# The second product of the second MoE with w2 as the stationary operand

## The chip, the cores and the metric

The kernel runs on one core of one Trainium2 chip. The metric is the device time of one execution in microseconds (us). The core has a matrix engine (PE, with its weight loads shown apart as PEld), a vector engine (DVE), a scalar engine (ACT), GpSimd (POOL) and a sync engine (SP), which here issues all DMAs.

## The reference

Three layers follow one another: a gated linear attention over 4 batches, 8 heads and 768 positions, a first MoE with one expert (d_ff 2048, gelu by a sigmoid), and a second MoE with four experts of width 1024. There are 3072 tokens of width 384. The change is in the second MoE:

```
p = domain_probs / (domain_probs.sum(-1, keepdims=True) + 1e-09)
for e in range(E):
    h = np.maximum(x @ w1[e], 0.0)
    out += p[:, e:e + 1] * (h @ w2[e])
```

The expert weight p is a number per token and expert. It can be multiplied into the result of the second product, as the reference writes it, or into the relu result before it.

## The kernel before

All products are made of a high and a low part of each float32 operand (both of type float32r), so that one product takes three: high by high, high by low, low by high. `split` makes the two parts: ACT copies the source into the high part, another engine subtracts it for the low part.

Three stages follow one another on PE. Stage one is attention in 24 chunks of 128 tokens, interleaved with the first steps of the first MoE and the conversion of its weights by a list written out by hand (`ORDER`); the entry `p` in it calls `pr_load`, which loads the expert weights and normalises them with four small DVE instructions. Stage two is the rest of the first MoE: 64 steps of `L1` (first product, L462) and `L2` (second product, L486), each 9 matmuls of 128 by 128 stationary and 512 tokens moving. Its results go to DRAM (`ydram`) and come back through `y_pieces`.

Stage three is the second MoE, the list `bsteps`: 8 units u (half an expert each, 512 of its 1024 hidden columns), in each 6 blocks j of 512 tokens, in each 4 slices ft of 128 hidden columns, so 192 steps. Step s runs `L3(u, j, ft)` and then `L4` of the step two before it (`lag = 2`; the operands wait in `pend`).

- `L3` (L514): 9 matmuls, w1 stationary, 512 tokens moving, into PSUM bank 3 or 4. Then ACT makes `hi` = relu (L520) and DVE makes `lo` = relu less `hi` (L521), in a ring of four pairs of tiles `G`.
- `L4` (L537): for each of four groups t of 128 tokens, 3 matmuls with `hi` or `lo` of these tokens as the stationary operand and 384 columns of w2 moving: 12 matmuls. The four results of a block have one PSUM bank each, out of a ring of six (`obanks`). With the last slice (ft = 3) DVE multiplies the result by p, a number per partition, and adds it to `acc` (L545 for u = 0, L547 after). In the last unit each group of 128 finished tokens is stored at once (L551).

`acc` holds tokens on the partitions and 384 columns along each. Things that run beside the steps are hung on step numbers by `at(i, fn)`: loads of the unit's weights (`unit_pieces`, L286, through the ring `RAW` of six tiles given out by `raw_tile`) and of `y`. SP issues in the order of its queue; a DMA that must wait for its tile holds up those behind it. The order within each engine's queue is laid down when the program is built, from the program order and the dependencies.

Of the kernel before, what the change touches and what calls it, by code (L numbers as in the profile page):

```python
# [8 lines left out]
F32 = mybir.dt.float32  # L9
F32R = mybir.dt.float32r  # L10
U32 = mybir.dt.uint32
ACTF = mybir.ActivationFunctionType
ALU = mybir.AluOpType
# [4 lines left out]


ORDER = """  # L20
00 10 01 11 20 30 l2 21 31 c0 c1 l3 c2 p c3 c7 c4 02 L c5 12 L L 22 M c6 L c8 03 32 l4 M 04 c9 M
L c10 13 M L 23 c11 M M 33 l5 c12 14 L L L 05 24 c13 34 15 L l6 M 06 L 25 M L M c14 35 M L l7 M
16 c15 L 26 M M 36 07 L L 17 27 M l8 37 M c16 c17 L M L 08 M L L M M L L c18 M L L c20 M M L L
l9 18 c19 M L M L M c23 M L L M M L c21 M L c22 09 M M M 28 38 L L 19 l10 L 010 M 29 39 L M 110
# [174 lines left out]
def attention_moe_moe2_kernel(  # L199
# [11 lines left out]
    nc = tc.nc  # L211
    NCH = qkf.shape[0]
    D = qkf.shape[2]
    NT, DM = out.shape
    NB = NT // 512
    CPB = 6
    NU = w1.shape[0]
    UPE = NU // probs.shape[2]
    KD = DM // 128
# [4 lines left out]
    dram = ctx.enter_context(tc.tile_pool(name="dram", bufs=1, space=bass.MemoryType.DRAM))  # L224
# [3 lines left out]
    arena = const.tile([128, 9224], F32, name="arena")  # L228
    WIDE = [const.tile([128, 1024], U32, name=f"wide{i}") for i in range(3)]
    bank = [psum.tile([128, 512], F32, name=f"bank{i}") for i in range(8)]  # L230
    pend_c = const.tile([128, NCH, 4], F32, name="pend_c")
    worst = const.tile([128, 1], F32, name="worst")
    flag = const.tile([1, 1], mybir.dt.int32, name="flag")
    ydram = dram.tile([NB + 2, KD, 128, 512], F32, name="ydram")
    yrows = [[0, 1], [2, 3]] + [[j + 2] for j in range(2, NB)]

    ident = const.tile([128, 128], F32, name="ident")
# [6 lines left out]
    pr = const.tile([128, NT // 128, 4], F32, name="pr")  # L244
    prs = const.tile([128, NT // 128, 1], F32, name="prs")
# [21 lines left out]
    GF = [carve(512) for _ in range(2)]  # L267
    CV = [[const.tile([128, 512], F32, name=f"cv{i}{j}") for j in range(3)] for i in range(2)]
    RAW = CV[0] + CV[1]
    acc = arena[:, 0:NT // 128 * DM].rearrange("p (a b) -> p a b", b=DM)  # L270

    raw_n = [0]

    def raw_tile():
        raw_n[0] += 1
        return RAW[raw_n[0] % 6]

    def split(hi, lo, src, eng):
        nc.scalar.copy(out=hi, in_=src)  # L279
        eng.tensor_tensor(out=lo, in0=src, in1=hi.bitcast(F32), op=ALU.subtract)  # L280

    def load_split(hi, lo, *srcs):
        def go():
            r = [raw_tile() for _ in srcs]
            for t, src in zip(r, srcs):
                nc.sync.dma_start(out=t, in_=src)  # L286

            def later():
                if len(r) > 1:
                    nc.gpsimd.tensor_tensor(out=r[0], in0=r[0], in1=r[1], op=ALU.add)  # L290
                split(hi, lo, r[0], nc.vector)
            return later
        return go

    def unit_pieces(hi, lo, src):
        return [
            load_split(hi[:, 512 * i:512 * i + 512], lo[:, 512 * i:512 * i + 512],
                       src[:, 512 * i:512 * i + 512])
            for i in range(3)
        ]  # L300
# [200 lines left out]
    onum = [0]  # L501
    obanks = [5, 6, 7, 0, 1, 2]

    def L3(u, j, ft):
        s = step_n[0]
        step_n[0] += 1
        h = bank[3 + s % 2]
        whi, wlo = us[u % 2][0]
        yhi, ylo = ys[j]
        i = 0  # L510
        for w, y in ((whi, yhi), (whi, ylo), (wlo, yhi)):
            for k in range(KD):
                c0 = 512 * k + 128 * ft
                nc.tensor.matmul(  # L514
                    h, w[:, c0:c0 + 128], y[:, 512 * k:512 * k + 512],
                    start=(i == 0), stop=(i == 8),
                )
                i += 1
        hi, lo = G[2 * (s % 4)], G[2 * (s % 4) + 1]
        nc.scalar.activation(out=hi, in_=h, func=ACTF.Relu)  # L520
        nc.vector.scalar_tensor_tensor(  # L521
            out=lo, in0=h, scalar=0.0, in1=hi.bitcast(F32), op0=ALU.max, op1=ALU.subtract
        )
        pend.append((u, j, ft, hi, lo))

    cur = {}

    def L4():
        u, j, ft, hi, lo = pend.pop(0)
        whi, wlo = us[u % 2][1]  # L530
        for t in range(4):
            if ft == 0:
                cur[t] = bank[obanks[onum[0] % 6]][:, 0:DM]
                onum[0] += 1
            o = cur[t]
            for s, (h, w) in enumerate(((hi, whi), (lo, whi), (hi, wlo))):
                nc.tensor.matmul(  # L537
                    o, h[:, 128 * t:128 * t + 128], w[:, DM * ft:DM * ft + DM],
                    start=(ft == 0 and s == 0), stop=(ft == 3 and s == 2),
                )  # L540
            if ft == 3:
                i = 4 * j + t
                p = pr[:, i, u // UPE:u // UPE + 1]
                if u == 0:
                    nc.vector.tensor_scalar_mul(out=acc[:, i], in0=o, scalar1=p)  # L545
                else:
                    nc.vector.scalar_tensor_tensor(  # L547
                        out=acc[:, i], in0=o, scalar=p, in1=acc[:, i], op0=ALU.mult, op1=ALU.add
                    )
                if u == NU - 1:  # L550
                    nc.sync.dma_start(out=out[128 * i:128 * i + 128], in_=acc[:, i])  # L551


    if True:
# [12 lines left out]
        for t in s_bd:  # L567
# [4 lines left out]
            out=mask, in_=mask, pattern=[[1, 128]], compare_op=ALU.is_ge, fill=0.0,  # L572
# [3 lines left out]
        for g in range(4):  # L576
            for (hi, lo), w in ((win[g], w_in[g]), (wout[g], w_out[g])):
                for i in range(3):
                    c0 = slice(512 * i, 512 * i + 512)
# [7 lines left out]
        def weights(n):  # L587
            for _ in range(min(n, len(wq))):
                hi, lo, src = wq.pop(0)
                r = WIDE[wide_n[0] % 3]  # L590
                nc.sync.dma_start(out=r, in_=src.bitcast(U32))
                loaded.append((wide_n[0], hi, lo, r))
                wide_n[0] += 1
# [7 lines left out]
        def convert(n):  # L601
            for _ in range(min(n, len(loaded))):
                convert_a()
                weights(1)
                hi, lo, w = half.pop(0)
                split(hi, lo, w, engine("weight_lo", conv_n[0]))
                conv_n[0] += 1

        def pr_load():
            nc.sync.dma_start(out=pr, in_=probs)  # L610
            nc.vector.reduce_sum(out=prs, in_=pr, axis=mybir.AxisListType.X)
            nc.vector.tensor_scalar_add(out=prs, in0=prs, scalar1=1e-9)
            nc.vector.reciprocal(out=prs, in_=prs)
            nc.vector.tensor_tensor(
                out=pr, in0=pr, in1=prs.to_broadcast([128, NT // 128, 4]), op=ALU.mult
            )

        weights(3)
        for _ in range(12):
            nc.tensor.matmul(bank[4][:, 0:128], ident, ident, start=True, stop=True)  # L620
# [5 lines left out]
        for ev in ORDER:  # L626
            if ev[0] == "c":
                convert(1)
            elif ev == "p":
                pr_load()  # L630
            elif ev == "L":
                L1(*esteps.pop(0))
            elif ev == "M":
                L2()
            else:
                acts[ev[0]](int(ev[1:]))()
# [4 lines left out]
        def at(i, fn):  # L641
            side.setdefault(i, []).append(fn)
# [20 lines left out]
        def piece_at(i, go):  # L663
            cell = []
            at(i, lambda: cell.append(go()))
            at(i + 2, lambda: cell[0]())

        e = len(steps) - 16
        for i, go in enumerate(unit_pieces(*us[0][0], w1[0])):
            piece_at(e + i, go)  # L670
        for i, go in enumerate(unit_pieces(*us[0][1], w2[0])):
# [6 lines left out]
        for i, (j, f, t0, n) in enumerate(steps):  # L678
# [7 lines left out]
            out=worst, in_=pend_c, axis=mybir.AxisListType.XY, op=ALU.min  # L686
# [3 lines left out]
            out=worst[0:1], in_=bank[5][0:1, 0:128], axis=mybir.AxisListType.X, op=ALU.min  # L690
        )
        nc.vector.tensor_scalar(
            out=flag, in0=worst[0:1], scalar1=PMIN, scalar2=None, op0=ALU.is_le
# [7 lines left out]
        for u in range(1, NU):  # L701
            pieces = unit_pieces(*us[u % 2][0], w1[u]) + unit_pieces(*us[u % 2][1], w2[u])
            for i, go in enumerate(pieces):
                piece_at(24 * (u - 1) + 6 + 2 * i + (4 if u == 1 else 0), go)
        lag = 2
        for i, (u, j, ft) in enumerate(bsteps):
            L3(u, j, ft)
            for fn in side.pop(i, []):
                fn()
            if len(pend) > lag:  # L710
                if len(pend[0]) == 6:
                    L2()
                else:
                    L4()
        while pend:
            L4()
# [53 lines left out]
```

## Time and profile before

| | |
|---|---|
| median of 3 runs | 1359.32 us (1358.34 to 1360.66) |
| profiled execution | 1360.01 us |
| its span, first to last instruction | 1358.3 us |
| mean granted TensorE clock | 0.984 of full speed |
| first matmul of L514, last matmul of L537 | 543.43 us, 1351.13 us |

The columns of a timeline are start and duration in us, engine, line, operation, result from operands, count; what stands in brackets is the idle time of that engine before and what ended it. Neighbouring instructions of one group are merged in one line. A matmul's duration is longer than the distance to the next one, since matmuls overlap in the array: what a group of matmuls takes is the distance between the starts of two groups, not its duration.

### The profile page before, as it was taken

The page shows a single profiled execution, that of the slowest core. Times are in us where ns is not written, and L with a number is a line of the kernel's source. Part 1 is how long each engine was busy: PE and PEld are TensorE (multiplying, and loading weights), DVE is VectorE, ACT ScalarE, POOL GpSimd, SP SyncE. Part 2 cuts the span into 40 slices and gives each one's busy share as a digit, 9 for nine tenths or more (in the row PEclk, how much of TensorE's full clock was granted, in tenths as well). Part 3 has the DMA queues.
Part 4 walks back from the last instruction along what each step waited for, and adds up shares of the span by engine and source line. Part 5 has one row for each costly group of instructions (what it writes and reads, how often), then busy time and mean ns, then how long its engine had stood idle before and what let it go on. Part 6 is the DMA issues. An engine that isn't in the chain of part 4 may idle for free.

```text
span 1358.3 us, 19558 instructions
## 1 busy us (share of the span) xinstructions
PE 1319.4 (97%) x8297; PEld 1154.7 (85%) x8297; DVE 611.4 (45%) x971; ACT 375.2 (28%) x674; POOL 133.9 (10%) x153
## 2 busy tenths in 40 slices
PE   5887999999999999999999999999999999999997
PEld 4776787888888888899999999999999999999997
DVE  8998367656656354523323323323323333333222
ACT  4664443334333344312112112112112112111111
POOL 5554233101111020000000000000000000000000
PEclk7788999999999999999999999999999999999999
DMA  7454112212111041400100001001001000000111
GB/s 225 138 154 131 39 49 77 75 35 82 52 45 52 1 147 47 156 0 17 31 0 25 23 0 31 17 0 32 16 0 33 15 1 1 1 0 0 36 52 55
DMA packets 30577, 64.32 MB, mean 47 GB/s; under 512 B 4368, under 2 KB 7440, under 8 KB 30480
## 3 DMA queue, kind: packets, MB, share of 16 engines
q1 hardware_dynamic: 30480, 62.98, 15.5%
q8 instruction: 67, 1.10, 0.3%
q14 instruction: 30, 0.25, 0.1%
HBM read 51.95 MB, written 11.01 MB: 46 GB/s over the span
## 4 chain that ended last, share of the span: by engine, by line
PE 84%; DVE 0%; DVEq 0%; issue 0%
PE bank L537 30%; PE bank L514 29%; PE bank L462 11%; PE bank L486 11%; PE bank L436 2%; PE bank L369 1%; PE bank L365 0%; PE bank L397 0%; DVE arena L547 0%; DVEq L719 0%; PE bank L688 0%
## 5 line engine op out<-in xcount | busy, mean ns | idle before, releaser
L537 PE MATMUL bank<-r,g 128*128 128x384 f32 x2304 | 434.8, 337 | 0.0
L514 PE MATMUL bank<-r,r 128*128 128x512 f32 x1728 | 430.7, 393 | 0.0
L537 PEld LDWEIGHTS bank<-r,g 128*128 128x128 f32 x2304 | 409.6, 188 | 16.8
L514 PEld LDWEIGHTS bank<-r,r 128*128 128x128 f32 x1728 | 321.4, 188 | 58.7
L521 DVE SCALAR_TENSOR_TENSOR g<-bank,g 128x512 fp32r<-128x512 f32 x192 | 132.2, 688 | 364.3 <-ACT g L520 364.3
L520 ACT ACTIVATE g<-bank 128x512 fp32r<-128x512 f32 x192 | 114.6, 597 | 615.5 <-PE bank L514 614.7
L486 PE MATMUL bank<-g,r 128*128 128x512 f32 (+1 forms) x936 | 220.4, 381 | 7.5 <-DVE g L280 2.5
L462 PE MATMUL bank<-r,r 128*128 128x512 f32 (+1 forms) x936 | 222.2, 385 | 2.3 <-ACT r L279 1.3
L486 PEld LDWEIGHTS bank<-g,r 128*128 128x128 f32 x936 | 169.9, 193 | 43.7 <-DVE g L280 3.7
L462 PEld LDWEIGHTS bank<-r,r 128*128 128x128 f32 x936 | 168.6, 195 | 37.1 <-issue 1.6
L547 DVE SCALAR_TENSOR_TENSOR arena<-bank,pr,arena 128x384 f32<-128x384 f32 x168 | 95.5, 610 | 132.6 <-PE bank L537 132.6
L470 DVE SCALAR_TENSOR_TENSOR arena<-arena,bank 128x512 f32<-128x512 f32 (+1 forms) x104 | 66.0, 636 | 87.4 <-ACT arena L469 87.3
L469 ACT ACTIVATE arena<-bank 128x512 f32<-128x512 f32 (+1 forms) x104 | 58.6, 564 | 121.3 <-PE bank L462 120.7
L280 DVE TENSOR_TENSOR g<-arena,g 128x512 fp32r<-128x512 f32 (+1 forms) x96 | 69.4, 724 | 40.1 <-ACT g L279 39.1
L279 ACT CAST g<-arena 128x512 fp32r<-128x512 f32 (+1 forms) x104 | 60.9, 589 | 78.5 <-DVE arena L470 78.5
L280 DVE TENSOR_TENSOR r<-cv,r 128x512 fp32r<-128x512 f32 x84 | 61.4, 747 | 45.4 <-ACT r L279 28.4
L279 ACT CAST r<-cv 128x512 fp32r<-128x512 f32 x90 | 54.4, 619 | 82.7 <-POOL cv L50 26.7
L50 POOL TENSOR_TENSOR cv<-cv,cv 128x512 uint32<-128x512 uint32 x24 | 35.5, 1480 | 42.8 <-DVE cv L47 28.9
L369 PE MATMUL bank<-arena 48*128 48x128 f32 x384 | 34.8, 317 | 0.0
L348 DVE TENSOR_TENSOR_SCAN arena<-arena,ends 128x512 f32<-128x512 f32 x24 | 33.8, 1410 | 0.2
L369 PEld LDWEIGHTS bank<-arena 48*128 48x128 f32 x384 | 28.9, 214 | 5.3 <-issue 4.4
L352 POOL TENSOR_TENSOR arena<-arena 128x512 f32<-128x512 f32 x22 | 29.9, 1361 | 15.1 <-DMA arena<-in_qkf 15.1
(70 smaller groups left out, 494.8 us busy)
## 6 DMA issues: line engine op xcount, KB each, us to landing
cv<-in_w SPq DMA_DIRECT2D x48, 256.0 KB, 2.8
arena<-in_qkf SPq DMA_DIRECT2D x48, 192.0 KB, 3.8
arena<-in_v SPq DMA_DIRECT2D x24, 256.0 KB, 3.8
wide<-in_w_in SPq DMA_DIRECT2D x12, 512.0 KB, 4.7
wide<-in_w_out SPq DMA_DIRECT2D x12, 512.0 KB, 4.3
ydram<-cv SPq DMA_DIRECT2D x24, 256.0 KB, 2.2
cv<-ydram SPq DMA_DIRECT2D x24, 256.0 KB, 3.0
arena<-in_qkf SPq DMA_DIRECT2D x48, 96.0 KB, 3.6
```

Source lines behind the costliest of these rows:

```text
L279: nc.scalar.copy(out=hi, in_=src)
L280: eng.tensor_tensor(out=lo, in0=src, in1=hi.bitcast(F32), op=ALU.subtract)
L369: nc.tensor.matmul(ab(c)[1 + r][:, 128 * p:128 * p + 128], kt[64 * r:64 * r + D, p], qt[64 * r:64 * r + D, p], start=True, stop=True,)
L462: nc.tensor.matmul(h, w[:, c0:c0 + 128], x[:, 512 * k + t0:512 * k + t0 + n], start=(i == 0), stop=(i == 8),)
L469: nc.scalar.activation(out=th, in_=h, func=ACTF.Tanh, scale=0.851)
L470: nc.vector.scalar_tensor_tensor(out=gf, in0=th, scalar=1.0, in1=h, op0=ALU.add, op1=ALU.mult)
L486: nc.tensor.matmul(bank[d][:, t0:t0 + n], w[:, c0:c0 + 128], g, start=(f == f0 and s == 0 and t0 == 0), stop=(f == f1 and s == 2 and t0 + ...
L514: nc.tensor.matmul(h, w[:, c0:c0 + 128], y[:, 512 * k:512 * k + 512], start=(i == 0), stop=(i == 8),)
L520: nc.scalar.activation(out=hi, in_=h, func=ACTF.Relu)
L521: nc.vector.scalar_tensor_tensor(out=lo, in0=h, scalar=0.0, in1=hi.bitcast(F32), op0=ALU.max, op1=ALU.subtract)
L537: nc.tensor.matmul(o, h[:, 128 * t:128 * t + 128], w[:, DM * ft:DM * ft + DM], start=(ft == 0 and s == 0), stop=(ft == 3 and s == 2),)
L547: nc.vector.scalar_tensor_tensor(out=acc[:, i], in0=o, scalar=p, in1=acc[:, i], op0=ALU.mult, op1=ALU.add)
```

## The change

In all steps of stage three but the last four (the last block of the last unit), `L4` takes w2 as the stationary operand (128 hidden by 128 output columns) and the 512 tokens of `hi` or `lo` as the moving one: 9 matmuls into 3 banks. The result stands transposed, output columns on the partitions and tokens along them, so p can no longer be a number per partition. It is multiplied into the relu result instead: DVE makes `gf` = relu times p (p spread over all partitions in `wide(.., 0)`), then `split` makes `hi` on ACT and `lo` on DVE. `acc` is kept transposed, with a plain copy or add of 128 by 512.

`pr_make` takes the place of `pr_load`: the same four steps, a transpose on PE and a store to DRAM (`ptd`), at step 48 of 64 of stage two. `pb_load` fetches for each unit and block the 512 weights, repeated on 128 partitions, six steps before the block (48 DMAs).

In the last unit each finished block is turned back: per 128 output columns one DVE transpose of 32 by 32 blocks into a `RAW` tile and four DMAs of 32 partitions, whose runs in DRAM are 32 numbers (128 bytes) long. That is 12 DMAs for each of five blocks. The last block keeps the old form of `L4` (`L4_last`), for which its partial sum of seven units is turned the same way through DRAM (`last_turn` at step 176, 12 DMAs to `otd`; `last_load` at step 182).

```
-    nc.scalar.activation(out=hi, in_=h, func=ACTF.Relu)
+    gf = wide(s, 1)
     nc.vector.scalar_tensor_tensor(
-        out=lo, in0=h, scalar=0.0, in1=hi.bitcast(F32), op0=ALU.max, op1=ALU.subtract
+        out=gf, in0=h, scalar=0.0, in1=wide(NB * u + j, 0), op0=ALU.max, op1=ALU.mult
     )
+    split(hi, lo, gf, nc.vector)
...
+def turned(src, dst, k):
+    r = raw_tile()
+    nc.vector.transpose(r, src)
+    for a in range(4):
+        c0 = 128 * k + 32 * a
+        nc.sync.dma_start(
+            out=dst[:, c0:c0 + 32].rearrange("(b i) c -> i b c", i=32),
+            in_=r[32 * a:32 * a + 32].rearrange("i (b c) -> i b c", c=32),
+        )
...
 def L4():
     u, j, ft, hi, lo = pend.pop(0)
     whi, wlo = us[u % 2][1]
+    if u == NU - 1 and j == NB - 1:
+        L4_last(ft, hi, lo, whi, wlo)
+        return
+    for d in range(KD):
+        if ft == 0:
+            cur[d] = bank[obanks[onum[0] % 6]]
+            onum[0] += 1
+    for s, (w, h) in enumerate(((whi, hi), (whi, lo), (wlo, hi))):
+        for d in range(KD):
+            c0 = DM * ft + 128 * d
+            nc.tensor.matmul(
+                cur[d], w[:, c0:c0 + 128], h,
+                start=(ft == 0 and s == 0), stop=(ft == 3 and s == 2),
+            )
+    if ft < 3:
+        return
+    for d in range(KD):
+        a = acc[:, j, d]
+        if u == 0:
+            nc.vector.tensor_copy(out=a, in_=cur[d])
+        else:
+            nc.vector.tensor_tensor(out=a, in0=a, in1=cur[d], op=ALU.add)
+        if u == NU - 1:
+            turned(a, out[512 * j:512 * j + 512], d)
...
+def pr_make():
+    nc.sync.dma_start(out=pr, in_=probs)
+    nc.vector.reduce_sum(out=prs, in_=pr, axis=mybir.AxisListType.X)
+    nc.vector.tensor_scalar_add(out=prs, in0=prs, scalar1=1e-9)
+    nc.vector.reciprocal(out=prs, in_=prs)
...
+    nc.tensor.transpose(bank[6][0:4 * NT // 128, 0:128], pn, ident)
+    nc.scalar.copy(out=pt, in_=bank[6][0:4 * NT // 128, 0:128])
+    nc.sync.dma_start(out=ptd.rearrange("e (i t) -> (e i) t", t=128), in_=pt)
...
+def pb_load(u, j):
+    def go():
+        nc.sync.dma_start(
+            out=wide(NB * u + j, 0),
+            in_=ptd[u // UPE:u // UPE + 1, 512 * j:512 * j + 512].to_broadcast([128, 512]),
+        )
+    return go
...
+e = len(steps) - 16
+at(e, pr_make)
+for n in range(2):
+    at(e + 12 + n, pb_load(0, n))
...
+for n in range(2, NU * NB):
+    at(4 * n - 6, pb_load(n // NB, n % NB))
+at(4 * NU * NB - 16, last_turn)
+at(4 * NU * NB - 10, last_load)
```

## Rows read from the trace of the kernel before

**Rows 1.** Page, part 1: busy time of each engine.
```profile
PE 1319.4 (97%) x8297; PEld 1154.7 (85%) x8297; DVE 611.4 (45%) x971; ACT 375.2 (28%) x674; POOL 133.9 (10%) x153
```
**Rows 2.** Page, part 4: the chain that ended last, by engine and line.
```profile
PE bank L537 30%; PE bank L514 29%; PE bank L462 11%; PE bank L486 11%; PE bank L436 2%; PE bank L369 1%; PE bank L365 0%; PE bank L397 0%; DVE arena L547 0%; DVEq L719 0%; PE bank L688 0%
```
**Rows 3.** That chain in order of time: start us, us, engine, tile, line.
```profile
821.87 2.10 PE bank L537 x12
...
1181.92 2.10 PE bank L537 x12
```
**Rows 4.** Timeline of PE, 1001.0 to 1006.1: late in stage three.
```profile
1001.73 2.27 PE L537 MATMUL bank<-r,g 128*128 128x384 f32 x12
1003.84 2.24 PE L514 MATMUL bank<-r,r 128*128 128x512 f32 x9
1005.92 0.51 PE L537 MATMUL bank<-r,g 128*128 128x384 f32 x2
```
**Rows 5.** Timeline of PE, 547.6 to 556.0: stage two passes into stage three.
```profile
547.64 2.20 PE L514 MATMUL bank<-r,r 128*128 128x512 f32 x9
549.68 2.20 PE L486 MATMUL bank<-g,r 128*128 128x512 f32 x9
551.72 2.20 PE L514 MATMUL bank<-r,r 128*128 128x512 f32 x9
553.76 2.27 PE L537 MATMUL bank<-r,g 128*128 128x384 f32 x12
555.86 0.39 PE L514 MATMUL bank<-r,r 128*128 128x512 f32 x1
```
**Rows 6.** Windows: stretch, length; busy PE, PEld, DVE, ACT, POOL; clock, DMA share, GB/s.
```profile
0.00:34.00 34.00, 19.60 (x237) 17.02 (x238) 27.68 (x43) 15.81 (x30) 19.56 (x30) 0.80 0.75 225
1001.89:1006.07 4.18, 4.18 (x23) 3.79 (x22) 2.79 (x5) 0.60 (x1) 0.00 (x0) 1.00 0.00 0
1351.50:1355.00 3.50, 0.00 (x0) 0.00 (x0) 0.63 (x2) 0.00 (x0) 0.00 (x0) 1.00 0.66 226
```
**Rows 7.** Groups by line and shape: busy us, mean ns; idle before, releaser.
```profile
L521 DVE SCALAR_TENSOR_TENSOR g<-bank,g 128x512 fp32r<-128x512 f32 x192 | 132.2, 688 | 364.3 <-ACT g L520 364.3
L520 ACT ACTIVATE g<-bank 128x512 fp32r<-128x512 f32 x192 | 114.6, 597 | 615.5 <-PE bank L514 614.7 <-DVE r L280 0.7
L547 DVE SCALAR_TENSOR_TENSOR arena<-bank,pr,arena 128x384 f32<-128x384 f32 x168 | 95.5, 610 | 132.6 <-PE bank L537 132.6
...
L348 DVE TENSOR_TENSOR_SCAN arena<-arena,ends 128x512 f32<-128x512 f32 x24 | 33.8, 1410 | 0.2
```
**Rows 8.** Timeline of all engines, 524.0 to 528.3: after an L1 of stage two.
```profile
525.04 2.20 PE L486 MATMUL bank<-g,r 128*128 128x512 f32 x9
525.30 0.60 ACT L469 ACTIVATE arena<-bank 128x512 f32<-128x512 f32 x1 [2.10 <-PE bank L462]
...
527.50 0.68 DVE L280 TENSOR_TENSOR g<-arena,g 128x512 fp32r<-128x512 f32 x1
```
**Rows 9.** Groups by line and shape: the instructions of pr_load.
```profile
L613 DVE RECIPROCAL prs<-prs 128x24 f32<-128x24 f32 x1 | 0.3, 289 | 0.0
...
L614 DVE TENSOR_TENSOR pr<-pr,prs 128x96 f32<-128x96 f32 x1 | 0.2, 236 | 0.0
L611 DVE TENSOR_REDUCE prs<-pr 128x24 f32<-128x96 f32 x1 | 0.2, 221 | 0.0
...
L612 DVE TENSOR_SCALAR prs<-prs 128x24 f32<-128x24 f32 x1 | 0.2, 164 | 0.0
```
**Rows 10.** DMA issues: what, queue, count, KB each, median us to landing.
```profile
cv<-in_w SPq DMA_DIRECT2D x48, 256.0 KB, 2.8
...
out<-arena SPq DMA_DIRECT2D x24, 192.0 KB, 1.9
```
**Rows 11.** Line 551 by itself: min, median, max ns on SP's queue.
```profile
L551 SPq DMA_DIRECT2D out<-arena x24: 332/332/382, 1271.0 to 1352.4; - x24
```
**Rows 12.** Timeline, 1349.5 to 1358.3: the last results and stores.
```profile
1349.94 2.19 DVE L547 SCALAR_TENSOR_TENSOR arena<-bank,pr,arena 128x384 f32<-128x384 f32 x4 [3.38 <-PE bank L537]
1350.59 2.14 SPq L551 DMA_DIRECT2D out<-arena  x4
```

More of the change, by code (lines that the diff above doesn't have):

```diff
@@ L20 @@
 ORDER = """
-00 10 01 11 20 30 l2 21 31 c0 c1 l3 c2 p c3 c7 c4 02 L c5 12 L L 22 M c6 L c8 03 32 l4 M 04 c9 M
+00 10 01 11 20 30 l2 21 31 c0 c1 l3 c2 c3 c7 c4 02 L c5 12 L L 22 M c6 L c8 03 32 l4 M 04 c9 M
 L c10 13 M L 23 c11 M M 33 l5 c12 14 L L L 05 24 c13 34 15 L l6 M 06 L 25 M L M c14 35 M L l7 M
@@ L234, in attention_moe_moe2_kernel @@
     ydram = dram.tile([NB + 2, KD, 128, 512], F32, name="ydram")
+    ptd = dram.tile([4, NT], F32, name="ptd")
+    otd = dram.tile([512, DM], F32, name="otd")
     yrows = [[0, 1], [2, 3]] + [[j + 2] for j in range(2, NB)]
@@ L269, in attention_moe_moe2_kernel @@
     RAW = CV[0] + CV[1]
-    acc = arena[:, 0:NT // 128 * DM].rearrange("p (a b) -> p a b", b=DM)
+    acc = arena[:, 0:NB * KD * 512].rearrange("p (a b c) -> p a b c", b=KD, c=512)
     raw_n = [0]
@@ L502, in attention_moe_moe2_kernel, with wide @@
     obanks = [5, 6, 7, 0, 1, 2]
+    def wide(i, n):
+        return WIDE[i % 3].bitcast(F32)[:, 512 * n:512 * n + 512]
+    def pr_make():
[3 more added lines that the diff above has]
+        nc.vector.reciprocal(out=prs, in_=prs)
+        pn, pt = wide(2, 0)[:, 0:4 * NT // 128], wide(2, 1)[0:4 * NT // 128, 0:128]
+        nc.vector.tensor_tensor(
+            out=pn.rearrange("p (e i) -> p i e", e=4), in0=pr, in1=prs.to_broadcast([128, NT // 128, 4]),
+            op=ALU.mult,
+        )
[9 more added lines that the diff above has]
+        return go
     def L3(u, j, ft):
@@ L530, in L4, with last_turn, last_load, L4_last @@
         whi, wlo = us[u % 2][1]
+        if u == NU - 1 and j == NB - 1:
[11 more added lines that the diff above has]
+                    start=(ft == 0 and s == 0), stop=(ft == 3 and s == 2),
+                )
+        if ft < 3:
[8 more added lines that the diff above has]
+                turned(a, out[512 * j:512 * j + 512], d)
+    at_last = []
+    def last_turn():
+        for d in range(KD):
+            turned(acc[:, NB - 1, d], otd, d)
+    def last_load():
+        at_last.extend(arena[:, DM * t:DM * t + DM] for t in range(4))
+        for t in range(4):
+            nc.sync.dma_start(out=at_last[t], in_=otd[128 * t:128 * t + 128])
+    def L4_last(ft, hi, lo, whi, wlo):
         for t in range(4):
@@ L541, in L4 @@
             if ft == 3:
[L542 to L551, printed above, removed]
+                r = at_last[t]
+                i = 4 * (NB - 1) + t
+                nc.vector.tensor_tensor(out=r, in0=o, in1=r, op=ALU.add)
+                nc.sync.dma_start(out=out[128 * i:128 * i + 128], in_=r)
     if True:
@@ L607, in convert @@
                 conv_n[0] += 1
[L609 to L616, printed above, removed]
         weights(3)
@@ L628, in attention_moe_moe2_kernel @@
                 convert(1)
-            elif ev == "p":
-                pr_load()
             elif ev == "L":
```

## The prediction

> **What bounds the kernel now.** I read the page's busy times first. PE is busy 97% of the span and no other engine half of it [rows 1], but a busy PE is only a PE with something in its array, so the next view is the chain of work that ended last. There L537 and L514, the two products of the second MoE, hold 59% of the span, and vector work holds next to nothing [rows 2]. In order of time the chain repeats one step without a change: 86 steps lie between 821.87 and 1181.92, so one takes 360.05 / 86 = 4.187 us [rows 3]. PE's timeline splits it by the starts of its groups: 2.11 us for the 12 matmuls of L537 with 384 columns, 2.08 us for the 9 of L514 with 512 [rows 4]. In such a step PE is busy all 4.18 us at a granted clock of 1.00 (2.4 GHz), DVE 2.79 and ACT 0.60 us [rows 6]. So stage three is bound by the rate at which PE takes matmuls. Nothing else in it is worth time unless it stops PE.
>
> The two groups have the same columns: 9 x 512 = 12 x 384 = 4608. A change that keeps columns can only gain what each matmul costs beyond its columns. The passage from stage two to stage three shows this: for two steps L514 still stands beside L486, which already has the form that the change gives to the second product (weights stationary, 512 of the relu or gelu result moving, 9 matmuls into 3 banks). There both groups take 2.04 us (547.64, 549.68, 551.72), 227 ns a matmul; from the first L537 on it is 2.10 us [rows 5]. So L514 is 0.04 us dearer beside the 384-column form than beside the 512-column form, and L537 itself 0.07 us.
>
> A page of the Trainium skill, TensorE: Matmul & The Clock Gate, section "Wait — 56ns, not 53.3ns?", gives a warm matmul its columns at 2.4 GHz and about 2.5 ns. Three matmuls fewer a step would by that be 7.5 ns, an estimate of 1.4 us over 188 steps. The trace does not agree: 227 ns for 512 columns is 13 ns over the 213 ns of the columns.
>
> **The change part by part.**
>
> The product. 192 steps less the last four have the new form: 188. Each falls from 4.187 us to 2 x 2.04 = 4.08 us. That is 0.107 us, times 188 is 20.1 us, all on the path. I take the 4.08 since the same code of L3 ran at it beside the same shape of product. Bounds: if only L4 falls to 2.04 and L3 stays at 2.08, 0.07 x 188 = 13 us; more than 20 is excluded as both groups run at the best pitch seen.
>
> The operands. Now ACT 0.60 and DVE 0.69 us follow a finished L3; after the change DVE 0.69 (relu times p, costed as L521, which also reads the bank and one tile), ACT 0.60, DVE 0.69 [rows 7]. This chain of 2.0 us and hand-offs has four PE groups, 8.2 us, before L4 needs it, and the bank of L3 is free after its first link, earlier than now. Stage two carries a longer chain with the same lag: tanh, product, copy, difference, from 525.30 to 528.18, and its PE goes on without a gap [rows 8]. Cost nothing, covered by those groups. Without that cover it would be 0.7 us a step.
>
> DVE's load. Per block (4 steps) now 4 x 0.69 + 4 x 0.61 = 5.2 us; after it 8 x 0.69 and three adds of 512 columns at 0.69, 7.6 us of 16.3. Copies of unit weights come on top, as now. Nothing on the path.
>
> The spread weights. 48 loads of 256 KB; a load of that size lands in 2.8 us [rows 10], and the step number leaves six steps, 24 us. The tile that each one takes was last read three blocks before, by a step already past when the load comes up, so it does not hold SP's queue for the weight loads behind it. Nothing.
>
> The start. Four DVE instructions, 0.29 + 0.24 + 0.22 + 0.16 = 0.9 us [rows 9], leave a stretch where DVE is busy 27.7 of 34 us and PE 19.6 [rows 6]. DVE is the nearer bound there: between 0 and 0.9 us gained, I take 0.5. Their new place, step 48 of stage two, puts a PE transpose behind them. If PE stands right behind L2 of that step, it waits for the chain of the L1 before it (2.9 us [rows 8]) and these 0.9 us, with 2.0 us of L2 beside it: 1.8 us lost at most, none if the transpose is queued later. I take 0.9. ACT's copy and SP's store of it hold the weight loads behind them by about the same, which step 50 first needs: nothing.
>
> The turning back. DVE transposes of 128 x 512 are not in the trace. The nearest rows are 0.69 us for a pass over two operands and 1.41 us for a scan [rows 7]; I take 0.69, since it is a pass without a running value, and keep 1.41. A block of the last unit then has a burst of 3 x (0.69 + 0.69) = 4.1 us on DVE, with the next step's first link behind it 4.8 us, against the 6.1 us that PE runs before it needs that bank again: nothing. At 1.41 it is 7.0 us, 0.9 us late, six times with the partial sums: 5.4 us. I take 0.5.
>
> The stores. 72 DMAs, each of 512 runs of 128 bytes, 32 per DMA engine if spread over all 16: 2304 runs an engine. They have from the end of the last unit's first block to the last matmul, 18 steps and two products, 78 us. On SP a store takes 0.33 us whatever the size in the trace [rows 11]: 24 us of 78, and the last 12 have 12 us. On the engines the four last stores move 512 packets of 1536 bytes at a share of 0.66 of 3.5 us: 0.66 x 3.5 x 16 / 512 = 72 ns a packet [rows 6]. A run of 128 bytes then costs between 6 ns (by bytes) and 72 ns (by packets). I take 20: 46 us of 78, hidden. Unhidden, it would be added to the end.
>
> The end. L4_last makes the same matmuls, DVE passes and stores as now [rows 12]. Nothing.
>
> Sum: -20.1 - 0.5 + 0.9 + 0.5 = -19.2 us. The profiled execution took 1360.0 us, 1.7 around its span of 1358.3; so 1340.8. The median of the runs shown is 0.7 lower, 1359.3, and gives **1340.1**.
>
> **The rivals.**
>
> *Short runs fill the DMA engines (slower).* At 72 ns a run the 72 stores take 2304 x 0.072 = 166 us, 88 more than they have, and the end waits for the last of them: -19 + 88 = +69, **1428**. It decides from (78 + 19) / 2304 = 42 ns. For it: no run so short is in the trace. Against it: packets of one size cost about their bytes, and a price by packets needs a large fixed part. The Trainium skill speaks for it: DMA: Bandwidth & Descriptors, Specifications, says that below 512 bytes the engine reads, modifies and writes. Doubling my 20 ns for that, an estimate, gives 40, just under that point. No run here shows it.
>
> *SP becomes the bound at the end.* If issuing goes with the number of runs, 512 against 128 is 4 x 0.33 = 1.3 us, 72 of them 96 us, 18 more than 78. The gain is given back: **1359**. At 1.1 us still hidden.
>
> *L3 keeps its 2.08 us.* Gain 13 instead of 20: **1347**. Rows 5 speak against it.
>
> *Only columns count.* Both groups of a step keep their 9216 columns, so w2 as weights could bring the irregular pitch along and both groups still take 4.18 us together; less the 0.9 us at the start and a few tenths the gain is about 1, **1358**. Against it: L486 has the same form and runs at 2.04 us [rows 5]. It is what the rule of the page on TensorE quoted above comes to here.
>
> **How the numbers follow.** Forecast 0.74, L3 keeps its pitch 0.08, SP 0.06, columns 0.04, short runs 0.08. Under 0.2% (2.7 us) is about what a measurement of this kernel cannot tell from none. Faster is the first two and 0.02 of the SP case, where issuing is a little cheaper: 0.84. Same is the rest of SP less 0.01 and the columns: 0.07. Slower is the short runs and that 0.01: 0.09. The range starts at 1336.5: no wait at the new transpose, no late bursts, the full 0.9 at the start, and 2 us for the queues of stage one, which are laid down anew without their entry `p`. It reaches to 1350, which takes in the late DVE bursts (1345) and the L3 rival; 0.18 lies above.
>
> **What would show it.** Right: starts of L3 and L4 groups 2.04 us apart all through stage three, the step 4.08 us, no idle PE in the last unit, the last transposed store landed before the last matmul. Wrong: groups still at 2.08 to 2.11; idle PE released by DVE's `gf` or by a spread-weight load; SP's stores of `turned` at over 1 us each, or a DMA share near 1 from the last unit's first block on with a tail behind the last matmul longer than now.

## The result and the profile after

The changed kernel takes 1340.57 us (median of 4 runs, 1340.32 to 1342.46) where the kernel before takes 1358.93 (median of 4, the three of the table ahead and one more): a ratio of 0.9865, with a 95% interval of 0.9853 to 0.9876. Measured once more in a later set it was 0.9862 [0.9847, 0.9877]. The profiled execution took 1340.8 us and has a span of 1339.1, 19.2 less than before.

The page of the changed kernel, parts 1 and 4, against [rows 1, 2]:

```profile
PE 1298.7 (97%) x7734; PEld 1075.7 (80%) x7734; DVE 737.9 (55%) x1134; ACT 378.8 (28%) x675; POOL 136.1 (10%) x153
...
PE bank L541 29%; PE bank L579 29%; PE bank L464 11%; PE bank L488 11%; PE bank L438 2%; PE bank L371 1%; PE bank L612 1%; PE bank L367 0%; PE bank L399 0%; DVE cv L558 0%; DVE wide L548 0%; DVE arena L619 0%; DVE arena L590 0%; PE bank L749 0%; PE bank L519 0%
```

PE is as busy as before and has 563 matmuls fewer: three in each of 188 steps, less the one transpose that is new. DVE has 126.5 us more to do and is still not in the chain, but for traces: its L548 and L590 now appear, which the rest of this section comes to. L541 is the first product (L514 before), L579 the new second product (L537 before), L612 the old form in the last block.

The timeline of PE in the middle of stage three, against [rows 4]:

```profile
800.57 2.20 PE L579 MATMUL bank<-g,r 128*128 128x512 f32 x9
802.61 2.20 PE L541 MATMUL bank<-r,r 128*128 128x512 f32 x9
804.65 2.20 PE L579 MATMUL bank<-g,r 128*128 128x512 f32 x9
806.69 2.20 PE L541 MATMUL bank<-r,r 128*128 128x512 f32 x9
```

Read the starts: 2.04 us from each group to the next. The step is 4.08 us, and of the 191 distances from one L541 to the next all but the first and the last two have it. From the start of the first matmul of L541 (541.37) to that of the last of L612 (1332.03) there are 790.7 us, where the kernel before had 807.7 (543.43 to 1351.13): 17.0 us less. Another 2.1 us were gained before stage three began, and 0.1 behind the last matmul. These three make the 19.2.

The 17.0 are 188 steps x 0.107 = 20.1 less a loss of 3.0. The loss stands in one place, the timeline of DVE and PE just before the end (what stands in brackets is idle time and what ended it):

```profile
1308.53 2.20 PE L541 MATMUL bank<-r,r 128*128 128x512 f32 x9
...
1312.61 2.20 PE L541 MATMUL bank<-r,r 128*128 128x512 f32 x9
...
1314.65 2.20 PE L579 MATMUL bank<-g,r 128*128 128x512 f32 x9
1316.44 1.28 DVE L590 TENSOR_TENSOR arena<-arena,bank 128x512 f32<-128x512 f32 x2 [7.62 <-PE bank L579]
1317.64 1.30 DVE L558 STREAM_TRANSPOSE cv<-arena 128x512 f32<-128x512 f32 x2
1318.86 1.25 DVE L548 SCALAR_TENSOR_TENSOR wide<-bank,wide 128x512 f32<-128x512 f32 x2
...
1319.57 2.34 PE L541 MATMUL bank<-r,r 128*128 128x512 f32 x9 [2.72 <-DVE wide L548]
```

The first L541 of the last block ends near 1310.6, and its relu pass (L548) could start at once: the spread weights of this block were issued at 1292.55 and had landed at 1297.24. DVE stands idle for 7.62 us instead, since the next instruction in its queue is the add of block 4 (L590), which waits for the L579 that runs from 1314.65. The two relu passes come after two adds and two transposes, at 1318.86, and PE's next L541 needs the bank that the first of them frees. PE starts 2.9 us late. The relu passes were not slow; they were behind.

The new DVE and DMA groups of the changed kernel (groups by line and shape; DMA issues with KB each and median us to landing; line 561 on SP's queue, min, median, max ns):

```profile
L282 DVE TENSOR_TENSOR g<-wide,g 128x512 fp32r<-128x512 f32 x192 | 132.7, 691 | 130.6 <-ACT g L281 130.2
L548 DVE SCALAR_TENSOR_TENSOR wide<-bank,wide 128x512 f32<-128x512 f32 x192 | 132.4, 690 | 247.3 <-PE bank L541 241.4 <-DMA otd<-cv 3.9 <-DMA wide<-ptd 2.0
...
L558 DVE STREAM_TRANSPOSE cv<-arena 128x512 f32<-128x512 f32 x18 | 12.0, 690 | 0.0
```
```profile
wide<-ptd SPq DMA_DIRECT2D x48, 256.0 KB, 3.2
...
out<-cv SPq DMA_DIRECT2D x60, 64.0 KB, 2.0
```
```profile
L561 SPq DMA_DIRECT2D out<-cv x60: 315/502/1430, 1253.5 to 1324.5; - x60
```

And a window over the 12 stores of block 3, issued from 1302.06 to 1309.29 (length; busy PE, PEld, DVE, ACT, POOL; clock, DMA share, GB/s):

```profile
1301.00:1312.00 11.00, 11.00 (x50) 9.09 (x50) 6.07 (x10) 1.25 (x2) 0.00 (x0) 1.00 0.48 73
```

The 12 stores are 6144 runs of 128 bytes. With all other traffic of the window put down to them, 0.48 x 11 us x 16 engines / 6144 is 13.8 ns a run, so a block keeps the engines busy for 5.3 of its 16.3 us.

### The profile page after: what moved, and what is told of

Same layout as the page of the kernel before. It is cut to its first block, busy times and chain, and to the rows that moved or that the text cites. A ratio compares the mean times of both kernels' runs of the same rounds, so it can differ in the third digit from the quotient of the medians.

```text
span 1339.1 us, 18792 instructions
## 1 busy us (share of the span) xinstructions
PE 1298.7 (97%) x7734; PEld 1075.7 (80%) x7734; DVE 737.9 (55%) x1134; ACT 378.8 (28%) x675; POOL 136.1 (10%) x153
## 4 chain that ended last, share of the span: by engine, by line
PE 84%; DVE 0%; issue 0%; DVEq 0%
PE bank L541 29%; PE bank L579 29%; PE bank L464 11%; PE bank L488 11%; PE bank L438 2%; PE bank L371 1%; PE bank L612 1%; PE bank L367 0%; PE bank L399 0%; DVE cv L558 0%; DVE wide L548 0%; DVE arena L619 0%; DVE arena L590 0%; PE bank L749 0%; PE bank L519 0%
## 5 line engine op out<-in xcount | busy, mean ns | idle before, releaser
L541 PE MATMUL bank<-r,r 128*128 128x512 f32 x1728 | 423.2, 389 | 2.7 <-DVE wide L548 2.7
L579 PE MATMUL bank<-g,r 128*128 128x512 f32 x1692 | 414.0, 389 | 0.0
L541 PEld LDWEIGHTS bank<-r,r 128*128 128x128 f32 x1728 | 324.2, 188 | 70.5 <-DVE wide L548 3.1
L579 PEld LDWEIGHTS bank<-g,r 128*128 128x128 f32 x1692 | 317.6, 188 | 65.9
L281 ACT CAST g<-wide 128x512 fp32r<-128x512 f32 x192 | 119.4, 622 | 620.9 <-DVE wide L548 620.9
L548 DVE SCALAR_TENSOR_TENSOR wide<-bank,wide 128x512 f32<-128x512 f32 x192 | 132.4, 690 | 247.3 <-PE bank L541 241.4
L282 DVE TENSOR_TENSOR g<-wide,g 128x512 fp32r<-128x512 f32 x192 | 132.7, 691 | 130.6 <-ACT g L281 130.2
L488 PEld LDWEIGHTS bank<-g,r 128*128 128x128 f32 x936 | 170.2, 193 | 40.1 <-ACT r L281 2.5
L590 DVE TENSOR_TENSOR arena<-arena,bank 128x512 f32<-128x512 f32 x123 | 77.2, 680 | 7.9 <-PE bank L579 7.9
```

The source lines that it names most:

```text
L488: nc.tensor.matmul(bank[d][:, t0:t0 + n], w[:, c0:c0 + 128], g, start=(f == f0 and s == 0 and t0 == 0), stop=(f == f1 and s == 2 and t0 + ...
L541: nc.tensor.matmul(h, w[:, c0:c0 + 128], y[:, 512 * k:512 * k + 512], start=(i == 0), stop=(i == 8),)
L548: nc.vector.scalar_tensor_tensor(out=gf, in0=h, scalar=0.0, in1=wide(NB * u + j, 0), op0=ALU.max, op1=ALU.mult)
L579: nc.tensor.matmul(cur[d], w[:, c0:c0 + 128], h, start=(ft == 0 and s == 0), stop=(ft == 3 and s == 2),)
L590: nc.vector.tensor_tensor(out=a, in0=a, in1=cur[d], op=ALU.add)
```

## The experiments

### Why the old step was dearer than its columns

Of the 0.107 us a step, part must be three matmuls fewer. But 231 ns for each L514 beside 384-column matmuls, against 227 beside 512-column ones [rows 4, 5], is no cost of the second product itself. Three things distinguish the old L4: the width that it moves, the role of its operands (weights that ACT and DVE have just written), and the count of its matmuls. Three kernels set them one by one. The first, from the kernel before:

```diff
-        for t in range(4):
+        for t in range(3):
```

> The kernel before with one of the four token groups of L4 left out (a quarter of the output is not formed): 9 matmuls of 384 columns, with the relu parts as weights. What makes the uneven distances of the old step (L3 at 231 instead of 227 ns a matmul, the first of L4 at 175 to 185 instead of 173)? Theory width (384 moving between 512 moving) and theory role (weights that were just written by ACT and DVE): still uneven, L3 2.08 us, L4 9 x 173 = 1.56 to 1.59. Theory count (12 and 9 matmuls in a step): even, L3 2.04, L4 1.56.

The second, from that one (each of the 9 matmuls moves 512 columns of w2, from a start that stays inside the tile):

```diff
...
-                    o, h[:, 128 * t:128 * t + 128], w[:, DM * ft:DM * ft + DM],
+                    o, h[:, 128 * t:128 * t + 128], w[:, min(DM * ft, 1024):min(DM * ft, 1024) + 512],
...
```

> As g_384, but each matmul of L4 moves 512 columns of w2 (128 of them meaningless): 9 matmuls of 512 with the relu parts as weights. Theory width and theory count: even, L3 and L4 both 2.04 us. Theory role: uneven, L3 2.08 and L4 2.06 to 2.08.

The third, from the changed kernel:

```diff
-                    cur[d], w[:, c0:c0 + 128], h,
+                    cur[d][:, 0:DM], w[:, c0:c0 + 128], h[:, 0:DM],
...
```

> The changed kernel, whose L4 moves only 384 of the 512 tokens (128 tokens of each block are left out): 9 matmuls of 384 with w2 as weights. Theory width: uneven, L3 2.08 us, L4 1.56 to 1.59. Theory role and theory count: even, L3 2.04, L4 1.56.

Measured: 1259.8, 1337.6 and 1270.3 us, a single execution each. The times are those of shorter or longer work; the timelines of PE decide. g_384, g_512 and w_384 in this order:

```profile
801.01 2.24 PE L514 MATMUL bank<-r,r 128*128 128x512 f32 x9
803.09 1.75 PE L537 MATMUL bank<-r,g 128*128 128x384 f32 x9
804.68 0.63 PE L514 MATMUL bank<-r,r 128*128 128x512 f32 x2
```
```profile
800.13 1.07 PE L514 MATMUL bank<-r,r 128*128 128x512 f32 x4
801.04 2.20 PE L537 MATMUL bank<-r,g 128*128 128x512 f32 x9
803.08 2.20 PE L514 MATMUL bank<-r,r 128*128 128x512 f32 x9
```
```profile
800.45 1.75 PE L579 MATMUL bank<-g,r 128*128 128x384 f32 x9
802.04 2.24 PE L541 MATMUL bank<-r,r 128*128 128x512 f32 x9
804.12 1.05 PE L579 MATMUL bank<-g,r 128*128 128x384 f32 x5
```

In g_384 L3 takes 2.08 us and L4 1.59. g_512, with the old roles, 2.04 for L4 and, over the whole stage, steps of 4.08 us: as fast as the change. w_384, with the new roles, has L3 at 2.08 and L4 at 1.59 again. Count falls with g_384 (18 matmuls, uneven), role falls with both others. It is the width. The granted clock is 1.00 from 800 to 808 us in all three.

Whether 384 is dear by itself or only beside 512 took two more kernels, both from w_384. One moves 384 columns in L3 as well:

```diff
...
-                    h, w[:, c0:c0 + 128], y[:, 512 * k:512 * k + 512],
+                    h, w[:, c0:c0 + 128], y[:, 512 * k:512 * k + DM],
...
```

> As w_384, and L3 moves 384 columns too (128 tokens of each block are left out throughout). Theory mix (the uneven distances come from a short product between long ones): even, both groups 9 x 173 = 1.56 us. Rival (384 columns are uneven by themselves): both groups 1.58 us or more.

The other moves 256 in L4 (`h[:, 0:256]` for `h[:, 0:DM]`, and the bank and the add cut likewise):

> As w_384 with 256 columns moving in L4 (half of the tokens are left out). If a matmul costs its columns at 2.4 GHz and 13.3 ns (227 for 512, 173 for 384), L4 takes 9 x 120 = 1.08 us. Theory mix: L3 is uneven again, at 2.08 us or above, since the widths differ more. Rival (something about 384 alone): L3 2.04 us.

Measured: 1167.2 and 1171.6 us, again one execution each, at a granted clock of 1.00 from 800 to 808 us. all_384, then w_256, on PE:

```profile
800.20 1.72 PE L579 MATMUL bank<-g,r 128*128 128x384 f32 x9
801.75 1.72 PE L541 MATMUL bank<-r,r 128*128 128x384 f32 x9
803.32 1.72 PE L579 MATMUL bank<-g,r 128*128 128x384 f32 x9
804.88 0.33 PE L541 MATMUL bank<-r,r 128*128 128x384 f32 x1
```
```profile
800.19 2.00 PE L541 MATMUL bank<-r,r 128*128 128x512 f32 x8
802.02 1.24 PE L579 MATMUL bank<-g,r 128*128 128x256 f32 x9
803.10 2.23 PE L541 MATMUL bank<-r,r 128*128 128x512 f32 x9
```

With one width throughout, 384 is even: 1.56 us for 9, 173 ns each. With 256 in L4 it takes 1.07 us (median), 120 ns each but for the first at 113, and L3 is uneven again at 2.07 (median). So theory mix holds, and each even matmul here costs its columns at 2.4 GHz and 13.3 ns: 213.3 + 13.3 at 512, 160 + 13.3 at 384, 106.7 + 13.3 at 256. The expectation for w_256 had L3 at 2.08 or above; it is 2.07, so a greater difference of widths does not cost more; it costs less.

This divides the gain of a step. The old L4 takes 2.106 us for 12 matmuls and that of g_384 1.586 for 9 (medians): three more cost 0.520, which is 173 ns each, so what unevenness costs does not grow with their count. Three matmuls fewer at 13.3 ns are 0.040 us, 7.5 us over 188 steps; the other 0.067 us, 12.5 us, are the evenness of one width.

### The gap before the last block

> The changed kernel, with the spread weights of the very last block in a tile of their own (floor, unused by then), loaded from step 100. Theory: the 2.9 us that PE stands idle before the last L3 come from DVE's queue, in which the adds of block 4 stand ahead of the first two relu passes of block 5, because the planner expected the load of these weights late; with the load early the relu passes stand first, the gap is gone and the step before last takes 4.08 us: 1337.6. Rival: PE would wait there anyway, for a bank or for the RAW tiles that the stores hold: 1340.6 as now.

```diff
     def wide(i, n):
+        if n == 0 and i == NU * NB - 1:
+            return floor
         return WIDE[i % 3].bitcast(F32)[:, 512 * n:512 * n + 512]
...
-            at(4 * n - 6, pb_load(n // NB, n % NB))
+            at(4 * n - 6 if n < NU * NB - 1 else 100, pb_load(n // NB, n % NB))
```

Measured: 1337.28 us, ratio to before 0.9834 [0.982, 0.9847]. DVE and PE of own_last in the same place:

```profile
1309.59 0.69 DVE L550 SCALAR_TENSOR_TENSOR wide<-bank,floor 128x512 f32<-128x512 f32 x1 [1.96 <-PE bank L543]
...
1313.67 0.69 DVE L550 SCALAR_TENSOR_TENSOR wide<-bank,floor 128x512 f32<-128x512 f32 x1 [1.96 <-PE bank L543]
...
1315.71 1.28 DVE L592 TENSOR_TENSOR arena<-arena,bank 128x512 f32<-128x512 f32 x2
```
```profile
1311.43 2.20 PE L543 MATMUL bank<-r,r 128*128 128x512 f32 x9
1313.47 2.20 PE L581 MATMUL bank<-g,r 128*128 128x512 f32 x9
1315.51 2.20 PE L543 MATMUL bank<-r,r 128*128 128x512 f32 x9
```

Both relu passes now start as soon as their L3 ends, ahead of the adds, and PE runs through. From the start of the first matmul of the stage to that of the last there are 787.6 us instead of 790.7. As the difference is near what runs scatter by, it was measured again beside the changed kernel:

> own_last once more, in one call with the changed kernel itself (the next run), so that both are compared with the same runs of the kernel before. Theory (the gap in DVE's queue is worth 2.9 us): about 3 us under the changed kernel. Rival (the 3.3 us between the first two calls were mostly chance): under 1.5 us.

> The changed kernel without an edit, beside own_last: 1340.6 as before by either theory; the difference to own_last tells.

Measured: 0.9842 [0.9829, 0.9856] against 0.9862 [0.9847, 0.9877]; by the medians 1337.70 against 1339.72. The ratios differ by 0.0020, 2.7 us; their intervals overlap, and it is the traces that show it: 787.6 against 790.7 us in both profiled executions of each. The first theory holds as to the gap: with the relu passes first, PE has nothing else to wait for there. That DVE's queue had its order because the load was expected late is inferred from what the edit does. It is shown that the order changes with the load, whose time and tile the edit changes together; which of the two did it was not separated.

### The stores of short runs

> As own_last, but the 60 stores of the turned blocks are left out (the DVE transposes stay; the first 2560 tokens of the output are not written). Theory: the stores of 128-byte runs are hidden, 13 ns a run on the DMA engines and 0.55 us each on SP: same time as own_last within 0.5 us. Rival: they cost something at the end, through SP's queue or the DMA engines: 1 to 5 us faster than own_last.

From own_last:

```diff
-                turned(a, out[512 * j:512 * j + 512], d)
+                nc.vector.transpose(raw_tile(), a)
```

Measured: 1338.67 us, 0.9845 [0.9832, 0.9859]. It is no faster than own_last; from the first to the last matmul both take 787.6 us. In stage three the stores cost PE nothing. By the medians it is 1.4 us slower. The two profiled executions are 2.2 us apart, and that lies outside stage three: it began 1.0 us later, which is within what it differs by from one execution to another, and the end behind the last matmul was 1.3 us longer, 7.8 us where the executions without doubled stores otherwise have 6.2 to 6.8. What made this end longer was not followed up.

> As own_last, with each of the 60 stores issued twice (the second into a scratch tensor). Theory: the limit is SP's issue, 0.55 us each: 24 a block are 13.2 us of 16.3, and only the last block's group, which has some 12 us to the last result, holds up the final stores: 0 to 4 us slower than own_last. Rival (short runs fill the DMA engines, as in the prediction): 132 stores of 32 runs an engine at 42 ns or more would be 177 us of 78: over 50 us slower. By the 13 ns of the trace they are 55 us and hidden.

Also from own_last:

```diff
...
-            nc.sync.dma_start(
-                out=dst[:, c0:c0 + 32].rearrange("(b i) c -> i b c", i=32),
-                in_=r[32 * a:32 * a + 32].rearrange("i (b c) -> i b c", c=32),
-            )
+            for o in (dst, *more):
+                nc.sync.dma_start(
+                    out=o[:, c0:c0 + 32].rearrange("(b i) c -> i b c", i=32),
+                    in_=r[32 * a:32 * a + 32].rearrange("i (b c) -> i b c", c=32),
+                )
...
```

Measured: 1354.89 us, 0.996 [0.9944, 0.9975]: 17.6 us over own_last, between what theory and rival had. SP, PE and DVE of own_twice, a window, and what SP waited for from 1250 to 1336 us (us in all, times, longest):

```profile
1298.55 0.50 SPq L528 DMA_DIRECT2D wide<-ptd  x1
...
1345.43 1.91 SPq L624 DMA_DIRECT2D out<-arena  x4
```
```profile
1299.55 2.20 PE L583 MATMUL bank<-g,r 128*128 128x512 f32 x9
1305.66 3.91 PE L544 MATMUL bank<-r,r 128*128 128x512 f32 x9 [3.91 <-DVE wide L551]
```
```profile
1301.33 1.88 DVE L594 TENSOR_TENSOR arena<-arena,bank 128x512 f32<-128x512 f32 x3 [6.41 <-PE bank L583]
1303.13 1.89 DVE L561 STREAM_TRANSPOSE cv<-arena 128x512 f32<-128x512 f32 x3
1304.95 1.25 DVE L551 SCALAR_TENSOR_TENSOR wide<-bank,wide 128x512 f32<-128x512 f32 x2
```
```profile
1298.00:1347.00 49.00, 34.44 (x155) 29.13 (x153) 20.21 (x32) 4.95 (x8) 0.00 (x0) 0.89 0.76 128
```
```profile
SPq L565 <- DVE cv L561: 21.8, 4, 8.0
```

SP is occupied almost without a break from 1298 to 1347 and the DMA engines are not (share 0.76). The last matmul starts at 1336.0, the last results leave SP at 1345.4: the end behind the last matmul is 17.4 us instead of 6.6. And at steps 185 and 186 PE loses 5.8 us, in part in the way seen before: the spread weights of block 4 are issued only at 1298.55, behind stores, and land at 1302.26, which is late this time, and DVE has the adds of the block before ahead of the relu passes, which come at 1304.95. So at the end the limit is SP's issue, as the theory had it, but the theory counted the issue alone and left out the waits in its queue: SP stood waiting for DVE's transposes (L561), once for 8.0 us, and the late groups piled up. The rival's price, 42 ns a run or more, is not the one measured (13.8 ns above), and its 50 us or more did not come.

### The start

> The kernel before, with the loading and normalising of the expert weights (four DVE instructions, one DMA) moved from the start to step 48 of stage two; nothing else. Theory: these instructions stand in the way of the DVE-bound start, and their removal is the 2.2 us that the changed kernel is ahead at the end of stage one: first matmul of the second MoE near 541.3 instead of 543.4 us, time near 1356.8. Rival: my step of the prediction, at most 0.9 us of DVE work can be gained: 1358.0 to 1358.9, and the rest of the 2.2 us came in another way.

```diff
-00 10 01 11 20 30 l2 21 31 c0 c1 l3 c2 p c3 c7 c4 02 L c5 12 L L 22 M c6 L c8 03 32 l4 M 04 c9 M
+00 10 01 11 20 30 l2 21 31 c0 c1 l3 c2 c3 c7 c4 02 L c5 12 L L 22 M c6 L c8 03 32 l4 M 04 c9 M
...
         e = len(steps) - 16
+        at(e, pr_load)
```

Measured: 1356.22 us, 0.9975 [0.9964, 0.9986]. PE of p_late where stage three begins:

```profile
540.12 0.27 PE L689 MATMUL bank<-ident,worst 128*1 128x128 f32 x1
540.14 2.33 PE L514 MATMUL bank<-r,r 128*128 128x512 f32 x9
```

Stage three begins at 540.1, where the kernel before had 543.4: the theory's 541.3, and a little more. A single execution says less here than it seems, though. In the profiles of this study stage three begins between 541.8 and 543.4 in the three executions with the early `p`, and between 540.1 and 542.6 in the ten without it. The means, 542.9 and 541.1, are 1.8 apart. The ratio of the runs, 0.9975, is 3.4 us (1.9 to 4.9). Removing 0.9 us of DVE work gains more than 0.9 us. The edit also takes a DMA out of the start and has all queues laid down anew; by which of these, and by which waits, was not followed up.

## Why the prediction was right

The forecast was 1340.1; 1340.57 was measured. Point by point, with the profiled execution's 19.2 us:

- *The product*, -20.1: exact, 188 steps at 4.08 us. The reason was right so far as it went: L514 beside L486 [rows 5] showed what both groups would cost. That it was the width and not the roles was open then; g_512 and w_384 showed it. The rivals "L3 keeps its 2.08" and "only columns count" fell with the first rows after.
- *Operands and DVE's load*, nothing: right. The relu pass and the difference took 0.69 us each, as costed, and no L4 waits for its operands.
- *The spread weights*, nothing: they land in 3.2 us, in time, and DVE waits for them 2.0 us in all, PE never. But own_last, which changes only the last of these loads, gets 3.0 us back, so this term had a price by way of the order in DVE's queue.
- *The start*, -0.5 with -0.9 at most: too small. Stage three begins 2.1 us earlier in the profile, with the new transpose's loss in it; p_late gained 3.4 (1.9 to 4.9). The step that failed is the bound: it took the work of the removed instructions for the most that could be gained, in a stretch whose queues are laid down anew without them. Only the lower end of the range had 2 us for that.
- *The transpose on PE*, +0.9: too large, 0.14. It takes 0.03 us between an L2 and an L1 that loses 0.11 us, and PE does not wait for the DVE steps before it:

```profile
473.88 2.20 PE L488 MATMUL bank<-g,r 128*128 128x512 f32 x9
475.92 0.27 PE L519 MATMUL bank<-ident,wide 128*96 128x128 f32 x1
475.95 2.31 PE L464 MATMUL bank<-r,r 128*128 128x512 f32 x9
478.10 2.20 PE L488 MATMUL bank<-g,r 128*128 128x512 f32 x9
```

- *The turning back*, +0.5 with 5.4 at most: 3.0 us, within the bounds, but not from a slow transpose. That took 0.69 us, as assumed. The prediction asked how long DVE's burst is and not where it stands in the queue: adds that wait for PE stood ahead of relu passes that were ready. So one of the prediction's own signs of being wrong, idle PE released by DVE's `gf`, did come: 2.72 us, once.
- *The stores*, nothing: right, with 13.8 ns a run where 20 was taken. SP's 0.33 us was too low: [rows 11] have it for one size alone, 128 runs of 1536 bytes; with 512 runs a store takes 0.50 behind another one, and the 72 took 37 us of the 78. That is far from the 1.3 us of the SP rival, as 13.8 ns is from the 42 of the short runs.

So the product, which is nearly all of the gain, came out for the reason given. That the sum came within 0.5 us is luck: two errors of opposite sign cancel, 2.5 us at the start with the transpose (0.4 lost by the forecast, 2.1 gained) and 2.5 too little lost at the end.

The Trainium skill, TensorE: Matmul & The Clock Gate, section "Wait — 56ns, not 53.3ns?", gives a warm matmul about 2.5 ns beyond its columns; by it, as an estimate, three matmuls fewer were worth 1.4 us. This case's traces do not agree: the fixed part is 13.3 ns at all three widths. Of the stores, a run of 128 bytes took 13.8 ns against 72 for 1536 bytes [rows 6], somewhat over twice its share by bytes (6.0 ns). The Trainium skill, DMA: Bandwidth & Descriptors, Specifications, says that below 512 bytes the engine reads, modifies and writes; no run here shows whether it does.

## What to carry to other kernels

When two matmul streams alternate, give them the same moving width and make it the widest: here a 384-column product between 512-column ones cost 0.040 us a step for its three extra matmuls and 0.067 for the unevenness, most of which fell on the other product. A short stretch of a trace in which the streams already stand in the new combination tells the new pitch better than any rule. And when an engine's queue gets work that waits for a slow partner (an add that waits for the end of a product), look at what is queued behind it: here the order turned round with a single load, which had landed 13 us before its use.

## What was not expected of the hardware

In these mixes of widths most of the penalty does not fall on the short matmuls. With 384 columns in L4, the 9 matmuls of L3 lose 0.041 us together and those of L4 0.026; with 256, L4 loses nothing against 9 x 120 ns and L3 0.027. The starts of single matmuls say more (medians from 700 to 1000 us): beside 384, the nine of L3 come at 224 to 236 ns, the first six of L4 at 171 to 185, and the rest of L4 at an even 173, with the same numbers within 1 ns in the kernel before, in g_384 and in w_384. Beside 256, only the first five of L3 are uneven (228 to 236) and the others are at 226 to 227. So the unevenness begins where a long matmul follows a short one and dies out, after 15 matmuls or after 5. It is the same in nearly every step, and it is gone when both widths are 384 or both 512. What in the engine makes it was not found.

The issue of a 512-run store on SP takes 0.32 us after a pause and 0.50 behind another one, 0.55 from one to the next. So 132 of them, 72 us of issue, were the bound at the end of own_twice, while the DMA engines had on average a quarter of their time left (share 0.76).
